# One core: windowed attention and a gated feed-forward layer, its hand-written order of steps replaced by another order of the same steps

## The chip, the cores and the metric

The kernel runs on one core of a Trainium2 chip. The core has a matrix engine (PE, with weight loads listed as PEld), a vector engine (DVE), a scalar engine (ACT), a general engine (POOL) and a queue that requests transfers between device memory and the on-chip memory (SP). Each works through its own instructions in order; they wait for each other by semaphores. The metric is the device time of one execution in microseconds (us), lower is better.

## What is computed

Four batches, 8 heads, 768 positions, 64 values a head. The attention sees the first 4 positions (the sinks) and a window of 128; behind it stands a gated layer of 512 to 1536 to 512.

```python
scores = scale * np.matmul(q, k.transpose(0, 1, 3, 2))
keep = is_sink | in_window
scores = np.where(keep, scores, -1000000000.0)
a = np.exp(scores - max); a = a / (sum + 1e-09)
x = np.matmul(a, v)                                   # 3072 x 512 over all batches
out = (np.maximum(x @ w_gate, 0) * (x @ w_val)) @ w_out
```

## The kernel before

The work is written as small steps, and one text, ORDER, lists all 1039 of them in the order in which they are issued. A step is a name and numbers (`G.0.1.5`); a table, OPS, maps the name to a function. The program issues exactly in this order (`tc.manual_schedule()`), and every engine's queue is what falls to it out of the list. Waits come from data and buffers alone.

Heads go in pairs: pair i (0 to 15) is batch i // 4, heads 2(i % 4) and the next. The steps, with the engine that runs them:

- Requests (SP): `hk.0.h`, `hq.0.h` load half h of keys and queries of pair 0, `kl.i` and `ql.i` those of pair i (384 KB each), `v.w.j` block j of the values of two pairs (w = i // 2; 128 KB, block 6 is 14 rows), `gl.c`, `xl.c`, `ol.c` one of six chunks of w_gate, w_val, w_out (512 KB each). `tk.i`, `tq.i` transpose keys and queries by DMA. `p`, `o` store results. A load into a buffer waits until the buffer's last reader is done: three buffers for keys and for queries, two for values, six of 512 KB for weights and results (`ws`; chunk c of w_gate is in buffer 2c mod 6, of w_val in 2c + 1 mod 6, of w_out in 6 + c mod 6).
- Constants: `sF`, `sE` (memsets on DVE; `sE` clears padding, ones and block 6 of the value buffers), `sI` (identity) and `sM` (bands of the mask) on POOL, `mk.g` and `mb.g` (masks on DVE), `P.n` (n idle matmuls on PE).
- Casts to bf16: `hc`, `kc`, `qc`, `c`, `f`, `gc`, `xc`, `oc` on POOL; with a capital letter (`kC`, `qC`, `cA`, `fA`, `gC`, `xC`, `oC`) and `hE` on ACT; `hD` on DVE. `f` and `fA` copy the sinks' rows.
- Transposes on PE: `HK`, `HQ` (halves of pair 0), `TK.i`, `TQ.i`; their copies out of PSUM `ha`, `hX`, `ka`, `kb`, `qA`, `qB` on ACT and `hx`, `hg`, `kd`, `ke`, `qa`, `qb` on DVE. Pairs 6 and up are transposed by DMA; `od.i` then arranges keys on POOL.
- Scores: `S.i.g` for a third g of the rows (64 rows of PE at a time, two heads beside each other); for pairs 0 to 3 `b.i.g` first adds the mask by a matmul and `B.i.g` the scores. `E.i.g` is the exponential (ACT), `M.i.g` the mask as a product (DVE).
- `Vd.i` sums (PE, 32-column tiles), `t`, `r`, `s`/`sa` (ACT), `R.i` bring the reciprocal of the sums to every row (DVE). `Va.i.part` multiplies by the values (PE, 32-column tiles; part is a column half), `x.i.part` scales into xT (DVE).
- Feed-forward, for batch b, column half g and 128 of the inner width m: `G.b.g.m` and `W.b.g.m` (PE, four matmuls each, line 502) with w_gate and w_val, `u` the relu (ACT, line 509), `h` the product (DVE, line 514). `F.b.t.m0.m1` is the down-projection of 128 rows (PE, line 524), `y` its copy (ACT), `Z.3.5` the last tile in three parts.

PSUM is four pairs of banks; `take` gives a step the pair that has been free longest in the order, so the order sets who waits for whose copy. Four batches follow each other: while PE does the feed-forward of batch b, the attention of batch b + 1 is woven in. PE's matmuls have three forms of tile: 128x128, 64 rows (scores) and 32 columns (`Vd`, `Va`).

In the order before, the first requests are hk.0.0 hk.0.1 hq.0.0 hq.0.1 kl.1 ql.1 v.0.0 v.0.6 kl.2 ql.2, and gl.2 stands ahead of v.1.5 and v.1.4.

Of the kernel before, what the change touches and what calls it, by code (L numbers as in the profile page):

```python
# [55 lines left out]
G.1.1.4 tk.8 y.0.5 x.6.0 G.1.1.5 kl.11 qc.10 u.1.1.5 kc.10 W.1.1.5 v.4.6 W.1.1.4 h.1.1.5 kl.12 tk.10 y.0.4 W.1.1.11
u.1.1.4 G.1.1.3 h.1.1.4 W.1.1.3 u.1.1.11 v.5.1 G.1.0.9 h.1.1.11 kc.11 G.1.0.0 u.1.1.3 G.1.0.7 u.1.0.0 h.1.1.3 G.1.1.0
u.1.1.0 W.1.0.7 W.1.1.0 u.1.0.9 h.1.1.0 u.1.0.7 G.1.1.10 W.1.0.9 h.1.0.9 h.1.0.7 W.1.0.0 W.1.1.10 od.9 v.5.2 u.1.1.10
G.1.1.8 W.1.1.8 h.1.1.10 G.1.0.4 u.1.1.8 W.1.0.4 tq.10 G.1.1.9 h.1.0.0 h.1.1.8 od.8 c.4.2.4 u.1.1.9 u.1.0.4 G.1.0.2
h.1.0.4 G.1.1.7 W.1.1.9 W.1.1.7 u.1.1.7 u.1.0.2 tq.9 h.1.1.9 v.5.5 W.1.0.2 v.4.0 S.8.0 h.1.1.7 h.1.0.2 S.8.2 S.8.1  # L60
G.1.0.10 W.1.0.10 E.8.2 u.1.0.10 h.1.0.10 E.8.1 G.1.0.11 v.4.1 u.1.0.11 W.1.0.11 h.1.0.11 M.8.2 c.5.2.4 G.1.1.2 S.9.2
E.8.0 S.9.0 S.9.1 v.5.0 W.1.1.2 E.9.2 E.9.0 G.1.0.3 E.9.1 W.1.0.3 M.8.0 M.9.2 od.10 ql.11 u.1.0.3 tk.11 v.4.4 G.1.0.1
G.1.1.1 u.1.1.2 M.9.1 h.1.1.2 W.1.0.1 h.1.0.3 u.1.0.1 ql.13 G.1.0.8 G.1.1.6 W.1.1.1 W.1.1.6 h.1.0.1 u.1.1.1 h.1.1.1
kC.12 G.1.0.5 W.1.0.5 qC.11 G.1.0.6 u.1.0.5 c.4.4.7 W.1.0.8 v.5.4 c.5.0.2 u.1.1.6 fA.4.3 M.9.0 M.8.1 u.1.0.8 ql.12
c.4.0.2 h.1.0.5 W.1.0.6 h.1.1.6 tq.11 h.1.0.8 u.1.0.6 h.1.0.6 S.10.0 S.10.1 E.10.0 S.10.2 E.10.1 Vd.8 kl.13 Vd.9
F.1.2.0.8 E.10.2 od.11 F.1.3.0.8 t.4 F.1.3.8.12 S.11.1 kl.14 r.4 S.11.0 S.11.2 s.4 M.10.0 cA.5.4.7 R.9 R.8 F.1.2.8.12
fA.4.5 E.11.1 M.11.1 ql.14 f.4.1 E.11.2 p.0.1 F.1.0.0.8 f.5.3 E.11.0 M.10.1 qC.12 M.10.2 f.5.1 M.11.0 M.11.2 y.1.2
y.1.3 f.5.5 v.6.3 kl.15 F.1.0.8.12 Vd.10 Va.9.0 tk.12 Va.8.0 Va.8.1 x.9.0 Vd.11 Va.9.1 F.1.1.0.8 t.5 F.1.4.0.8 v.6.4
r.5 s.5 qC.13 x.8.0 v.6.2 kc.13 F.1.1.8.12 tq.12 y.1.0 y.1.1 v.6.6 F.1.5.0.8 x.8.1 F.1.5.8.12 Va.11.0 Va.10.0 c.6.2.4
Va.11.1 R.11 x.9.1 Va.10.1 R.10 F.1.4.8.12 v.6.5 x.10.0 x.11.0 x.11.1 G.2.0.7 u.2.0.7 od.12 x.10.1 v.6.1 tk.13 W.2.0.7  # L70
G.2.0.0 G.2.0.3 W.2.0.0 y.1.4 u.2.0.0 h.2.0.0 W.2.0.3 p.0.0 G.2.1.9 c.6.4.7 h.2.0.7 kc.15 u.2.0.3 G.2.0.11 qc.14 y.1.5
sA G.2.1.4 W.2.1.9 u.2.0.11 od.13 v.7.4 u.2.1.4 W.2.0.11 tq.13 h.2.0.11 kC.14 h.2.0.3 u.2.1.9 p.1.0 G.2.1.3 v.7.2
h.2.1.9 W.2.1.4 h.2.1.4 G.2.1.8 G.2.0.4 tk.15 u.2.0.4 u.2.1.3 u.2.1.8 v.7.5 p.1.1 v.6.0 G.2.0.8 tk.14 W.2.1.3 tq.14
h.2.1.3 W.2.1.8 W.2.0.8 u.2.0.8 h.2.0.8 c.6.0.2 W.2.0.4 S.13.2 h.2.1.8 h.2.0.4 S.12.1 E.13.2 G.2.1.2 u.2.1.2 v.7.1
W.2.1.2 h.2.1.2 G.2.1.1 ql.15 E.12.1 S.13.1 S.13.0 W.2.1.1 v.7.6 G.2.0.1 E.13.0 E.13.1 u.2.0.1 G.2.0.9 od.15 W.2.0.1
# [536 lines left out]
```

## Time and profile before

| | |
|---|---|
| median of three runs | 242.9 us (242.54 to 243.76) |
| profiled execution, span | 242.4 us (no other time of its own is listed) |
| busy: PE, PEld, DVE, ACT, POOL | 234.9, 137.1, 133.2, 131.6, 57.9 us |
| DMA | 39.0 MB, mean 161 GB/s |
| granted clock of PE | full in all 40 slices |

The span runs from the first to the last instruction of the one execution that was profiled. Busy times count an engine's instructions; a matmul's end is modelled, so the distance from start to start says more than its length. The page cuts the span in 40 slices of 6.1 us and gives tenths of busy time. The chain is followed back from the last instruction to what released each step. In a timeline row stand start, length, engine, line, operation, output and inputs, count, and in brackets the idle time before it with what ended it. In a window's row stand the window, its length, busy time of PE, PEld, DVE, ACT and POOL with counts, the clock, the DMA engines' share and GB/s.

### The profile page before, as it was taken

The page shows a single profiled execution, that of the slowest core. Times are in us where ns is not written, and L with a number is a line of the kernel's source. Part 1 is how long each engine was busy: PE and PEld are TensorE (multiplying, and loading weights), DVE is VectorE, ACT ScalarE, POOL GpSimd, SP SyncE. Part 2 cuts the span into 40 slices and gives each one's busy share as a digit, 9 for nine tenths or more (in the row PEclk, how much of TensorE's full clock was granted, in tenths as well). Part 3 has the DMA queues.
Part 4 walks back from the last instruction along what each step waited for, and adds up shares of the span by engine and source line. Part 5 has one row for each costly group of instructions (what it writes and reads, how often), then busy time and mean ns, then how long its engine had stood idle before and what let it go on. Part 6 is the DMA issues. An engine that isn't in the chain of part 4 may idle for free.

```text
span 242.4 us, 5536 instructions
## 1 busy us (share of the span) xinstructions
PE 234.9 (97%) x2213; PEld 137.1 (57%) x2213; DVE 133.2 (55%) x268; ACT 131.6 (54%) x254; POOL 57.9 (24%) x106
## 2 busy tenths in 40 slices
PE   7899989999999999999999999999999999999995
...
GB/s 168 329 279 280 346 341 255 314 316 309 182 227 187 167 230 199 191 166 38 224 219 187 206 135 153 23 143 3 0 3 3 29 318 4 0 0 0 3 130 130
DMA packets 88329, 39.00 MB, mean 161 GB/s; under 512 B 73712, under 2 KB 83824, under 8 KB 88304
## 3 DMA queue, kind: packets, MB, share of 16 engines
...
q8 instruction: 17, 0.28, 0.5%
...
## 4 chain that ended last, share of the span: by engine, by line
PE 80%; SPq 7%; DMA 7%; issue 5%; ACT 0%; DVE 0%
PE pp L502 49%; PE pp L524 22%; DMA ws<-in_moe_w_gate_dram 4%; SPq L237 4%; PE pp L404 3%; PE pp L449 3%; DMA vf<-in_v_dram 3%; PE pp L438 2%; SPq L241 2%; SPq L231 1%; SPq L217 1%; PE pp L329 0%; ACT wg L270 0%; DVE ws L549 0%
## 5 line engine op out<-in xcount | busy, mean ns | idle before, releaser
L514 DVE TENSOR_TENSOR hT<-gs,pp 128x378 bf16<-128x378 f32 (+1 forms) x96 | 50.7, 552 | 75.3 <-PE pp L502 52.0
L509 ACT ACTIVATE gs<-pp 128x378 f32<-128x378 f32 (+1 forms) x96 | 44.2, 494 | 53.9 <-PE pp L502 41.5
L502 PE MATMUL pp<-xT,wg 128*128 128x378 bf16 (+1 forms) x384 | 72.4, 326 | 1.0 <-ACT wg L270 1.0
L502 PE MATMUL pp<-xT,wv 128*128 128x378 bf16 (+1 forms) x384 | 71.9, 326 | 0.0
L524 PE MATMUL pp<-wo,hT 128*128 128x512 bf16 x276 | 62.3, 379 | 0.0
L502 PEld LDWEIGHTS <-wg 128*128 128x128 bf16 x384 | 36.9, 98 | 26.7 <-ACT wg L270 1.4
L502 PEld LDWEIGHTS <-wv 128*128 128x128 bf16 x384 | 37.4, 98 | 25.3 <-issue 0.4
L419 ACT ACTIVATE ee<-pp 128x1010 bf16<-128x1010 f32 (+2 forms) x48 | 43.9, 961 | 11.2 <-PE pp L404 10.9
L524 PEld LDWEIGHTS <-hT 128*128 128x128 bf16 x276 | 26.1, 98 | 30.5 <-issue 0.4
L530 ACT COPY ws<-pp 128x512 f32<-128x512 f32 x23 | 13.1, 589 | 26.0 <-PE pp L524 26.0
L425 DVE TENSOR_TENSOR ee<-ee,msk 128x1014 bf16<-128x1014 bf16 (+2 forms) x36 | 25.5, 747 | 1.6 <-ACT ee L419 1.5
L485 DVE STREAM_TRANSPOSE R<-r 128x832 f32<-128x832 f32 x16 | 16.4, 1037 | 5.2 <-ACT r L477 4.7
L262 POOL CAST vn<-vf 128x512 bf16<-128x512 f32 (+1 forms) x18 | 12.6, 715 | 23.7 <-DMA vf<-in_v_dram 23.7
L491 DVE TENSOR_TENSOR xT<-pp,R 128x390 bf16<-128x390 f32 (+1 forms) x32 | 16.1, 546 | 3.8 <-PE pp L449 3.3
L404 PE MATMUL pp<-qT,kE 64*128 64x255 bf16 (+4 forms) x164 | 13.4, 248 | 0.2 <-ACT qT L355 0.2
L449 PE MATMUL pp<-ee,vn 128*32 128x252 bf16 (+6 forms) x512 | 12.6, 241 | 0.1
L254 POOL CAST qn<-qf 128x768 bf16<-128x768 f32 x11 | 9.4, 858 | 13.1 <-DMA qf<-in_q_dram 12.2
L449 PEld LDWEIGHTS <-vn 128*32 128x32 bf16 x512 | 10.9, 96 | 1.9 <-issue 1.1
L290 POOL COPY kO<-kE 128x372 bf16<-128x372 bf16 x10 | 6.0, 596 | 24.5 <-PE pp L404 20.4
L251 POOL CAST kn<-kf 128x768 bf16<-128x768 f32 x11 | 9.1, 824 | 8.1 <-DMA kf<-in_k_dram 7.4
L460 DVE STREAM_TRANSPOSE t<-pp 128x832 f32<-128x832 f32 (+1 forms) x10 | 8.7, 867 | 4.0 <-PE pp L438 3.2
L404 PEld LDWEIGHTS <-kE 64*128 64x128 bf16 x164 | 6.6, 93 | 7.1 <-issue 5.5
...
## 6 DMA issues: line engine op xcount, KB each, us to landing
...
out_dram<-ws SPq DMA_DIRECT2D x10, 512.0 KB, 3.3
ws<-in_moe_w_gate_dram SPq DMA_DIRECT2D x6, 512.0 KB, 7.8
ws<-in_moe_w_val_dram SPq DMA_DIRECT2D x6, 512.0 KB, 7.8
ws<-in_moe_w_out_dram SPq DMA_DIRECT2D x6, 512.0 KB, 5.2
...
```

What stands on the lines that cost most here:

```text
L262: copy(dst[:, j0:j1, :, :].rearrange("p j h d -> p (j h d)"), src[:, j0:j1, :, :].rearrange("p j h d -> p (j h d)"))
L404: mm = lambda h, c0, c1, lhs, rhs, st: on(("S", i, g), "PE", 1 << h, nc.tensor.matmul(out=ps[:, h, c0:c1], lhsT=lhs, rhs=rhs, start=st, st ...
L419: on(("S", i, g), "ACT", 3, nc.scalar.activation(ee[i % NE][:, g, :, 0:n], use(("S", i, g))[:, :, 0:n], Act.Exp, bias=0.0, scale=scale))
L425: nc.vector.tensor_tensor(x, x, msk[:, g, 0:n].unsqueeze(1).to_broadcast([128, 2, n]), op=Alu.mult)
L449: on(("V", i), "PE", 1 << part, nc.tensor.matmul(out=ps[p0:p0 + 32, part, o0:o0 + c1 - c0], lhsT=vn[w % NVN][:, j, h0 + h, d:d + 32], rhs= ...
L485: nc.vector.transpose(out=R[:].rearrange("p s (c e) -> p (s c) e", e=32), in_=r.rearrange("p s c -> p (s c)").unsqueeze(2).to_broadcast([1 ...
L491: on(("V", i), "DVE", 1 << part, nc.vector.tensor_tensor(xT[b % 2][:, p, c0:c1], use(("V", i))[:, part, 0:c1 - c0], held_r[i][:, part, 0:c ...
L502: on(("F", b, g, m), "PE", 1 << which, nc.tensor.matmul(out=ps[:, which, 0:c1 - c0], lhsT=(wg, wv)[which][:, ko, m * 128:(m + 1) * 128], r ...
L509: on(("F", b, g, m), "ACT", 1, nc.scalar.activation(x[:, 0:n], use(("F", b, g, m))[:, 0, 0:n], Act.Relu, bias=0.0, scale=1.0))
L514: on(("F", b, g, m), "DVE", 2, nc.vector.tensor_tensor(hT[:, m, c0:c1], gs[b, g, m][:, 0:c1 - c0], use(("F", b, g, m))[:, 1, 0:c1 - c0], o ...
L524: on(name, "PE", 1 << t % 2, nc.tensor.matmul(out=ps[:, t % 2, :], lhsT=hT[:, m, t * 128:(t + 1) * 128], rhs=wo[:, m, :], start=m == 0, st ...
L530: on(name, "ACT", 1 << t % 2, act_copy(staged(b, t), use(name)[:, t % 2, :]))
```

## The change

ORDER is replaced. No step is added or taken away and no step moves to another engine; every queue gets its steps in another order. The first requests are now hk.0.1 hq.0.1 hk.0.0 hq.0.0 v.0.0 ql.1 v.0.6 kl.1 kl.2 ql.2 kl.3 ql.3, all blocks of the first batch's values stand ahead of gl.2, and steps of the same form stand together on PE in more places. The core of it, as far as the last value block of batch 1:

```diff
@@ -28,69 +28,69 @@
 ZCUT = (0, 256, 384, 512)
 
 ORDER = """
...
-hk.0.0 sF sE P.40 sM hk.0.1 hq.0.0 mk.0 hc.0.0 mk.1 mk.2 hq.0.1 sI mb.1 b.0.1 mb.0 HK.0.0 hE.0.0 HQ.0.0 b.0.0 mb.2 P.3
-hD.0.1 kl.1 ql.1 v.0.0 v.0.6 hc.0.1 HK.0.1 kl.2 ql.2 HQ.0.1 v.0.2 ha.0.0 hx.0.0 hX.0.1 hg.0.1 B.0.0 b.0.2 B.0.1 B.0.2
-E.0.0 kc.1 v.0.1 kl.3 b.1.1 TK.1 ql.3 qc.1 kc.2 qc.2 ke.1 TQ.1 E.0.1 v.0.3 E.0.2 kc.3 b.1.2 qB.1 qA.1 qc.3 v.0.5 Vd.0
-kd.1 t.0.0 B.1.2 B.1.1 v.1.6 TK.2 r.0.0 b.1.0 TQ.2 kl.4 E.1.2 c.0.0.2 B.1.0 ke.2 E.1.1 s.0.0 c.0.2.4 f.0.1 f.0.3 qb.2
-b.2.0 ka.2 qa.2 v.1.1 b.2.2 kc.4 E.1.0 R.0 B.2.2 v.0.4 Vd.1 B.2.0 TK.3 v.1.3 E.2.2 ql.4 c.0.4.7 TQ.3 E.2.0 b.2.1 qA.3
-v.1.0 qB.3 t.0.1 B.2.1 r.0.1 v.1.2 b.3.0 b.3.2 kd.3 f.0.5 s.0.1 ke.3 qc.4 E.2.1 B.3.0 Vd.2 R.1 E.3.0 B.3.2 t.1.2 r.1.2
-c.1.0.2 gl.2 c.1.2.4 Va.0.0 E.3.2 f.1.3 Va.0.1 b.3.1 v.1.5 B.3.1 TK.4 v.1.4 TQ.4 Va.1.0 x.0.1 sa.1.2 gl.1 E.3.1 f.1.1
-x.0.0 c.1.4.7 f.1.5 qA.4 R.2 kb.4 x.1.0 Vd.3 t.1.3 P.2 r.1.3 ka.4 xl.2 xl.1 qB.4 Va.2.0 xl.0 Va.1.1 v.2.1 sa.1.3 x.1.1
-S.4.1 gc.4 S.4.0 gc.5 x.2.0 E.4.0 Va.3.0 gC.2 R.3 x.3.0 Va.2.1 x.2.1 Va.3.1 xc.5 x.3.1 gl.0 S.4.2 G.0.0.4 E.4.2
-G.0.0.2 E.4.1 xc.4 u.0.0.4 G.0.0.5 kl.5 u.0.0.2 u.0.0.5 gl.5 W.0.0.5 G.0.1.5 W.0.0.4 gc.3 M.4.1 gl.4 xC.2 h.0.0.5 xl.5
-W.0.0.2 G.0.1.2 xC.0 gC.0 h.0.0.2 u.0.1.5 h.0.0.4 u.0.1.2 gc.11 W.0.1.2 v.3.1 W.0.1.5 h.0.1.2 xC.1 G.0.1.4 u.0.1.4
-xc.3 v.2.0 gC.10 G.0.1.0 gc.9 G.0.1.3 h.0.1.5 W.0.1.4 u.0.1.0 W.0.1.0 h.0.1.0 u.0.1.3 G.0.0.3 G.0.0.11 xc.10 ql.5
-W.0.0.3 h.0.1.4 kC.5 W.0.1.3 gC.1 TK.5 u.0.0.3 h.0.0.3 xl.4 G.0.0.0 h.0.1.3 kl.7 xl.3 ke.5 W.0.0.0 xC.11 u.0.0.11
-W.0.0.11 qc.5 G.0.1.11 TQ.5 ka.5 h.0.0.11 G.0.1.1 v.2.6 gl.3 qb.5 qa.5 u.0.0.0 gC.8 ol.2 h.0.0.0 W.0.1.11 ql.6 W.0.1.1
-S.5.2 u.0.1.1 u.0.1.11 h.0.1.11 xC.9 S.5.0 h.0.1.1 S.5.1 G.0.1.10 ol.5 E.5.2 M.4.2 G.0.0.8 M.5.2 E.5.0 E.5.1 W.0.1.10
-G.0.0.10 G.0.1.9 W.0.1.9 xC.8 gc.6 u.0.1.10 xC.6 gc.7 u.0.1.9 W.0.0.10 u.0.0.10 h.0.1.9 h.0.1.10 G.0.0.1 kl.6 xc.7
-oc.2 ol.1 h.0.0.10 W.0.0.1 ol.3 G.0.0.9 G.0.1.8 u.0.0.1 h.0.0.1 u.0.0.9 G.0.0.6 qc.6 u.0.0.8 ol.0 W.0.0.9 tq.6 oc.0
-ql.7 W.0.0.8 ol.4 h.0.0.8 kC.6 tk.6 G.0.1.7 h.0.0.9 u.0.0.6 M.5.0 G.0.1.6 W.0.1.6 v.2.4 oC.1 M.5.1 W.0.0.6 W.0.1.8
-u.0.1.6 h.0.0.6 G.0.0.7 h.0.1.6 oC.3 W.0.0.7 u.0.0.7 v.3.5 kc.7 u.0.1.7 M.4.0 cA.2.0.2 W.0.1.7 u.0.1.8 qc.7 oc.5
-h.0.1.7 v.2.2 h.0.0.7 tk.7 Vd.4 Vd.5 v.3.4 od.6 t.2 tq.7 v.2.5 oC.4 v.2.3 od.7 F.0.0.0.8 F.0.1.0.8 S.6.1 h.0.1.8 v.3.0
-E.6.1 S.6.2 S.6.0 r.2 E.6.0 v.3.3 sa.2 F.0.1.8.12 E.6.2 F.0.0.8.12 R.4 F.0.2.0.8 M.6.2 ql.8 c.2.4.7 c.2.2.4 y.0.1
-M.6.0 F.0.2.8.12 y.0.0 v.3.6 M.6.1 y.0.2 fA.2.3 v.3.2 f.2.1 c.3.2.4 S.7.1 E.7.1 S.7.0 kl.9 kl.8 S.7.2 F.0.3.0.8
-F.0.3.8.12 v.4.3 E.7.0 R.5 c.3.0.2 Vd.6 E.7.2 M.7.1 fA.2.5 Va.5.0 cA.3.4.7 Va.4.0 v.4.2 ql.9 y.0.3 M.7.0 fA.3.3 qc.8
-Va.4.1 M.7.2 f.3.1 x.5.0 Vd.7 t.3 f.3.5 x.4.1 F.0.4.0.8 Va.5.1 v.4.5 r.3 v.5.3 Va.7.0 Va.7.1 sa.3 x.5.1 Va.6.0 Va.6.1
-F.0.5.0.8 v.5.6 kc.9 F.0.5.8.12 R.6 x.4.0 R.7 tk.9 kc.8 x.7.0 x.6.1 x.7.1 F.0.4.8.12 qC.9 tq.8 kl.10 ql.10 G.1.1.11
...
+sI hk.0.1 sF sM mk.0 mb.0 hq.0.1 P.40 b.1.0 hk.0.0 hc.0.0 HK.0.0 hq.0.0 hE.0.0 b.0.0 mk.2 mb.2 v.0.0 P.3 hc.0.1 HK.0.1
+ql.1 qc.1 sE hD.0.1 v.0.6 ha.0.0 HQ.0.1 hX.0.1 mk.1 mb.1 HQ.0.0 hx.0.0 kl.1 b.0.2 kl.2 B.0.0 kc.1 hg.0.1 B.0.2 E.0.0
+E.0.2 kc.2 b.0.1 B.0.1 E.0.1 ql.2 b.1.1 qc.2 TK.1 TQ.1 kl.3 kd.1 Vd.0 qA.1 qB.1 ke.1 t.0.0 r.0.0 B.1.0 E.1.0 ql.3 P.2
+kc.3 TK.2 B.1.1 v.0.1 b.2.0 TQ.2 v.0.2 b.1.2 qc.3 B.1.2 ke.2 s.0.0 E.1.1 qb.2 b.2.2 v.0.3 ql.4 c.0.0.2 f.0.1 qa.2
+c.0.2.4 f.0.3 ka.2 B.2.2 B.2.0 R.0 v.1.6 E.1.2 E.2.2 Vd.1 t.0.1 E.2.0 TK.3 r.0.1 kd.3 s.0.1 v.0.4 qc.4 ke.3 TQ.3 qB.3
+b.2.1 B.2.1 v.0.5 b.3.2 qA.3 kl.4 b.3.0 v.1.1 B.3.0 R.1 E.2.1 B.3.2 E.3.0 Vd.2 t.1.2 r.1.2 c.0.4.7 Va.1.0 E.3.2 x.1.0
+Va.0.0 x.0.0 f.0.5 Va.0.1 b.3.1 B.3.1 sa.1.2 E.3.1 x.0.1 kc.4 v.1.0 v.1.2 TK.4 v.1.3 kb.4 ka.4 c.1.0.2 f.1.1 R.2
+c.1.2.4 f.1.3 v.1.5 v.1.4 c.1.4.7 f.1.5 TQ.4 gl.2 qA.4 gc.4 Va.1.1 x.1.1 Vd.3 xl.2 qB.4 t.1.3 r.1.3 Va.2.0 gl.1 x.2.0
+gc.5 Va.2.1 x.2.1 S.4.0 v.3.6 sa.1.3 E.4.0 S.4.2 E.4.2 Va.3.0 Va.3.1 xc.4 R.3 x.3.1 xl.1 S.4.1 x.3.0 M.4.2 G.0.1.5
+G.0.0.4 G.0.0.5 W.0.0.4 u.0.0.4 M.4.0 h.0.0.4 gl.0 xc.5 W.0.1.5 u.0.1.5 h.0.1.5 xl.0 gC.2 gl.5 G.0.1.4 E.4.1 kl.5 xl.5
+W.0.0.5 gc.3 ql.5 v.3.3 xC.2 G.0.1.3 xc.3 u.0.0.5 h.0.0.5 W.0.1.4 G.0.0.2 u.0.1.4 h.0.1.4 gc.11 G.0.1.2 gC.0 u.0.1.2
+v.2.0 W.0.1.2 h.0.1.2 xl.4 W.0.0.2 u.0.0.2 u.0.1.3 W.0.1.3 h.0.1.3 xC.0 G.0.1.0 G.0.0.3 u.0.0.3 W.0.0.3 h.0.0.3
+W.0.1.0 gC.10 G.0.0.0 qc.5 gC.1 h.0.0.2 W.0.0.0 gl.3 xc.10 G.0.0.11 kC.5 u.0.1.0 h.0.1.0 G.0.1.11 TK.5 xC.1 ke.5 xC.11
+W.0.1.11 u.0.1.11 u.0.0.0 xl.3 h.0.0.0 gc.6 u.0.0.11 TQ.5 gl.4 G.0.1.10 qb.5 qa.5 gc.7 h.0.1.11 W.0.0.11 W.0.1.10 ka.5
+S.5.2 xc.7 h.0.0.11 u.0.1.10 h.0.1.10 kl.7 ol.4 ol.5 S.5.0 E.5.2 S.5.1 ql.6 E.5.1 G.0.0.10 G.0.0.1 W.0.0.10 G.0.1.1
+W.0.1.1 xC.6 M.4.1 qc.6 W.0.0.1 M.5.1 u.0.0.1 E.5.0 gc.9 u.0.1.1 h.0.1.1 M.5.2 h.0.0.1 ol.0 v.2.3 gC.8 G.0.1.7 u.0.1.7
+oc.0 W.0.1.7 G.0.0.7 W.0.0.7 u.0.0.7 h.0.0.7 M.5.0 xC.9 G.0.0.6 W.0.0.6 ol.1 u.0.0.6 kl.6 h.0.1.7 xC.8 ol.3 G.0.1.6
+W.0.1.6 ol.2 G.0.1.9 ql.7 u.0.1.6 kc.7 u.0.1.9 h.0.1.6 Vd.4 Vd.5 h.0.0.6 G.0.1.8 u.0.0.10 h.0.0.10 oC.1 G.0.0.9
+W.0.0.9 kC.6 oc.2 tq.6 oC.3 tk.6 t.2 r.2 sa.2 R.5 W.0.1.9 W.0.1.8 v.2.4 G.0.0.8 W.0.0.8 h.0.1.9 u.0.1.8 F.0.0.0.8 oC.4
+tk.7 u.0.0.9 h.0.1.8 u.0.0.8 qc.7 F.0.1.0.8 oc.5 h.0.0.8 od.6 h.0.0.9 F.0.0.8.12 S.6.0 v.3.2 E.6.0 S.6.2 E.6.2 od.7
+S.6.1 F.0.1.8.12 M.6.2 F.0.2.0.8 F.0.2.8.12 v.2.1 cA.2.0.2 E.6.1 y.0.0 y.0.1 v.3.1 tq.7 S.7.0 v.3.0 E.7.0 c.3.0.2
+f.3.1 S.7.1 R.4 S.7.2 E.7.1 M.6.1 v.2.2 F.0.3.0.8 F.0.3.8.12 c.2.2.4 f.2.1 y.0.2 Va.5.0 v.3.4 v.2.6 c.3.2.4 v.2.5
+c.2.4.7 M.6.0 Va.4.0 v.3.5 M.7.1 v.4.1 ql.8 E.7.2 M.7.0 Va.7.0 fA.2.3 fA.2.5 x.5.0 M.7.2 y.0.3 Va.5.1 x.5.1 v.4.2
+cA.3.4.7 fA.3.3 Vd.6 Va.6.0 x.4.0 Va.4.1 x.4.1 Vd.7 t.3 r.3 sa.3 f.3.5 R.6 Va.6.1 x.6.1 Va.7.1 R.7 F.0.4.0.8 F.0.5.0.8
...
 """.split()
```

77 lines of the change are left out of this document (39 added, 38 removed).

## The prediction

> **What bounds the kernel now.** I read the page's shares and slices first, then the chain of waits, then the timelines of the engines over the first 40 us.
>
> ```profile
> span 242.4 us, 5536 instructions
> PE 234.9 (97%) x2213; PEld 137.1 (57%) x2213; DVE 133.2 (55%) x268; ACT 131.6 (54%) x254; POOL 57.9 (24%) x106
> PE   7899989999999999999999999999999999999995
> ```
>
> PE is busy 97%, and full from the seventh slice (36 us) on. Busy alone doesn't prove a limit; the chain does:
>
> ```profile
> 25.23 9.66 DMA ws<-in_moe_w_gate_dram
> 34.91 0.63 ACT wg L270
> 35.59 5.50 PE pp L502 x32
> 182.30 10.47 PE pp L524 x48
> 192.77 29.88 PE pp L502 x184
> ```
>
> From 35.59 us every piece up to the close is PE's. 184 projection matmuls in 29.88 us are 0.1624 us each, 48 of the down-projection in 10.47 are 0.218; the same rates hold throughout, so behind 35.59 there is PE work and changes of tile form, and no stall to remove. All that PE can lose or win otherwise lies before 35.59, where the first batch's attention runs and the weights arrive.
>
> ```profile
> 27.24 2.09 PE L502 MATMUL pp<-xT,wg 128*128 128x378 bf16 x12
> 35.59 1.60 PE L502 MATMUL pp<-xT,wg 128*128 128x390 bf16 x8 [1.03 <-ACT wg L270]
> ```
>
> The up-projection starts at 27.24. By 35.59 it has done 11 groups of four matmuls (G.0.0.4 to G.0.1.4 of the order): 44 x 0.1624 = 7.15 us of work in 8.35. So 1.2 us are lost, all at G.0.1.0, which waits for gl.0, the first 256 columns of w_gate (requested at 25.23, landed 34.89, cast by ACT).
>
> **The change, part by part.** The same 1039 steps stand in another order; I counted and walked them queue by queue.
>
> *Changes of form.* PE alternates 128x128 tiles, 64-row tiles (scores) and 32-column tiles (sums, values). Counted along the order, the changes go from 67 to 58; after the first up-projection group from 38 to 32. The price of one:
>
> ```profile
> 99.66 2.12 PE L502 MATMUL pp<-xT,wv 128*128 128x390 bf16 x12
> 101.72 0.28 PE L404 MATMUL pp<-qT,kE 64*128 64x253 bf16 x2
> L502 PE MATMUL pp<-xT,wv 128*128 128x390 bf16 x192 | 37.6, 328 | 0.0
> ```
>
> The last of the twelve starts at 99.66 + 2.12 - 0.33 = 101.45, its successor in the same form would start 0.165 later, at 101.62; the score starts at 101.72: 0.10 us. Six fewer on the full stretch: -0.6 us. The three fewer ahead of it fall where PE waits anyway: 0.
>
> *The weight wait.* In the new order G.0.1.0 has 14 groups ahead of it, not 11 (+2.0 us of PE work), and gl.0 has 0.65 MB less ahead of it in the request queue (xl.0 and v.2.1 go behind it). It is late no more: -1.2 us. The new v.3.6 ahead of xl.1 on SP waits until POOL has cast batch 0's last values.
>
> ```profile
> 25.07 0.82 POOL L262 CAST vn<-vf 128x768 bf16<-128x768 f32 x1 [1.48 <-DMA vf<-in_v_dram]
> 26.30 1.16 POOL L270 CAST wg<-ws 128x512 bf16<-128x512 f32 x2
> ws<-in_moe_w_gate_dram SPq DMA_DIRECT2D x6, 512.0 KB, 7.8
> ```
>
> That cast and its row of sinks end near 26.3; so xl.1 lands by 26.6 + 7.8 = 34.4, and is wanted eleven groups (7.1 us) after the start at 28.9 (below): 36.0. Covered by 1.6 us less a cast of 0.6.
>
> *The first requests.* This is where the new order pays. SP's new queue is hk.0.1, hq.0.1, hk.0.0, hq.0.0, v.0.0, ql.1, v.0.6, kl.1, kl.2, ql.2, kl.3, ql.3. v.0.6 overwrites rows that sE has cleared on DVE, so it waits for sE. sE ran at once; now it stands behind mk.0, mb.0, mk.2 and mb.2, and mk.0 waits for POOL's bands.
>
> ```profile
> 1.51 0.31 DVE L188 MEMSET kE<- 128x57 uint32 x4
> 1.86 0.55 DVE L191 MEMSET vf<- 128x256 f32 x2
> 3.49 0.16 DVE L198 MEMSET msk<- 4x126 bf16 x1 [0.84 <-POOL msk L179]
> 4.11 0.23 DVE L202 COPY msk<-msk 128x252 bf16<-128x252 bf16 x1
> 4.25 0.31 DVE L204 COPY msk<-msk 128x255 bf16<-128x255 bf16 x1
> 4.98 0.66 DVE L210 TENSOR_SCALAR mb<-msk 128x507 bf16<-128x507 bf16 x3
> 0.81 0.96 SPq L231 DMA_DIRECT2D kf<-in_k_dram  x2
> 2.83 0.47 SPq L217 DMA_DIRECT2D kf<-in_k_dram  x1
> 3.41 0.50 POOL L257 CAST kn<-kf 128x384 bf16<-128x384 f32 x1
> 8.76 0.83 POOL L251 CAST kn<-kf 128x768 bf16<-128x768 f32 x1 [3.83 <-DMA kf<-in_k_dram]
> 10.73 0.51 PE L329 MATMUL pp<-ident,qn 128*128 128x128 bf16 x6 [0.58 <-POOL qn L254]
> ```
>
> From 3.49: mk.0 0.6 (to 4.11), mb.0 and mb.2 a third of 0.66 each, mk.2's copies 0.75 (4.25 to 4.98, with waits 0.9), sE's kE and ones 0.4, the first vf 0.27: v.0.6 can go near 6.1, kl.1 at 6.6 instead of 2.83. Meanwhile the queue holds 1.3 MB. When does kl.1 land? It took 5.9 us (2.83 to 8.76) behind four half loads; the first half load, with nothing ahead, took 2.6 (0.81 to 3.41). A whole load is 0.2 MB more, 0.6 us at the 328 GB/s of 6 to 12 us (below). So 3.2 to 5.9 us, landing between 9.8 and 12.5; I take 4.3, landing at 10.9, nearer the lower end since little is ahead, while kl.2, ql.2 and kl.3 follow at 0.5 us and share the engines. Then the cast 0.83, TK.1 and TQ.1 0.35 each: TQ.1 ends at 12.4, against 11.24 (10.73 + 0.51). Delay 1.2 us. Does it pass on?
>
> ```profile
> 6.00:12.00 6.00, 4.90 (x66) 2.80 (x65) 2.87 (x9) 4.61 (x11) 2.04 (x3) 1.00 1.11 328
> 12.00:18.00 6.00, 5.64 (x78) 3.08 (x76) 5.59 (x17) 5.53 (x10) 3.90 (x6) 1.00 1.05 281
> 18.00:24.00 6.00, 5.85 (x119) 3.40 (x120) 5.64 (x14) 5.74 (x15) 5.43 (x11) 1.00 0.98 276
> 25.85 1.05 DVE L485 STREAM_TRANSPOSE R<-r 128x832 f32<-128x832 f32 x1
> 27.00 1.49 DVE L491 TENSOR_TENSOR xT<-pp,R 128x378 bf16<-128x378 f32 x3
> ```
>
> It does. From 12 us DVE (third column) and ACT (fourth) are busy over 92%, in nearly the old order: what starts late ends late. In addition x.2.1 now stands ahead of R.3 on DVE, and the first group is of the second column half, which needs x.3.1 behind R.3: 0.5 us (27.00's three take 1.49). Start of the up-projection: 27.24 + 1.2 + 0.5 = 28.9: +1.7 us. gl.2, whose casts took 26.30 to 27.46, has the last two values ahead of it and the later start; 1.4 us are covered. sI ahead of the bands fits POOL's idle 0.8 us; b.1.0 0.5 us sooner, hk.0.1 ahead of hk.0.0 and B.0.0 0.8 us later sit before ACT's wait for TQ.1: 0.
>
> The Trainium skill, "DMA: Bandwidth & Descriptors", section "Anatomy of one DMA", puts a load at about 2.0 us plus its bytes at 436 GB/s (fitted on another path): an estimated 2.9 us for kl.1, landing at 9.5, where it would delay nothing, and a sum of -0.3 where mine is +0.9. No load in these rows is that quick; by it the faster rival below would be near.
>
> *w_out.* ol.3 takes the staging buffer that xC.8 empties, xC.8 stands behind u.0.0.6 on ACT, and ol.2, ql.7 and both transposes stand behind ol.3 on SP. So ol.3 and ol.2 are requested only when PE has done G.0.0.6: 37 groups x 0.65 + 1.6 for transposes and scores after the start = 54.6, plus relu 0.5 and cast 0.6: 55.7 and 56.2.
>
> ```profile
> ws<-in_moe_w_out_dram SPq DMA_DIRECT2D x6, 512.0 KB, 5.2
> 57.97 1.46 POOL L274 CAST wo<-ws 128x1024 bf16<-128x1024 f32 x1 [6.02 <-DMA ws<-in_moe_w_out_dram]
> ```
>
> Landing 5.2 later and 1.46 of cast: 62.9. F.0.0 starts at 28.9 + 48 x 0.65 + 2.6 (transposes, scores, sums, changes) = 62.7 and uses that chunk four matmuls (0.9) later: covered by 0.7. With the gate weights' 7.8 us it would be late by 1.9. I take 0.3. tk.6 behind them lands in time for S.6.0 by under 1 us: 0.
>
> *Dense blocks.* Fewer changes mean that values and sums of four pairs stand in one block, with no down-projection between to cover DVE.
>
> ```profile
> 72.00:84.00 12.00, 11.98 (x200) 6.90 (x198) 11.30 (x17) 6.71 (x14) 5.03 (x7) 1.00 1.10 177
> L419 ACT ACTIVATE ee<-pp 128x1010 bf16<-128x1010 f32 (+2 forms) x48 | 43.9, 961 | 11.2 <-PE pp L404 10.9
> L425 DVE TENSOR_TENSOR ee<-ee,msk 128x1014 bf16<-128x1014 bf16 (+2 forms) x36 | 25.5, 747 | 1.6 <-ACT ee L419 1.5
> L485 DVE STREAM_TRANSPOSE R<-r 128x832 f32<-128x832 f32 x16 | 16.4, 1037 | 5.2 <-ACT r L477 4.7
> L491 DVE TENSOR_TENSOR xT<-pp,R 128x390 bf16<-128x390 f32 (+1 forms) x32 | 16.1, 546 | 3.8 <-PE pp L449 3.3
> 78.19 1.75 PE pp L449 x75
> ```
>
> Batch 1, from the end of S.7.0 to the next up-projection: PE has 0.5 of scores, 36 down-projections x 0.218 = 7.8, 128 value matmuls at 1.75/75 = 3.0, two sums 0.8, changes 0.3: 12.4 us. The other chain is two exponentials 1.9, three masks 2.2, six x's 3.3, t and r 1.5, ACT's copies of r 0.9, two R 2.1: 11.9, and some 0.5 of hand-overs. They are level, and DVE was busy 11.3 of 12 there already: the cover is gone, and what comes late shows in full. Three such blocks, 0 to 0.5 each: I take 0.5 in all. Everything else that moves (stores, casts, later loads) lies beside full PE: 0. The close is the same.
>
> **Sum.** -0.6 - 1.2 + 1.7 + 0.3 + 0.5 = +0.7; with 0.2 for weights that may now gate the start, +0.9. The span is 242.4, 0.5 under the median of 242.9; against the median 243.8.
>
> **Rivals.** *Late refill (slower).* kl.1 lands at 12.5, as slowly as before. Start +3.3, w_out +0.8, blocks +0.6: -1.8 + 4.7 = +2.9, 245.8. For it: the row 8.76; against: little is ahead. It decides from a landing after 11.3. *Quick refill (faster).* kl.1 lands at 9.8, start +0.6, no later stalls: -1.8 + 0.6 = -1.2, 241.7. For it: the first half load's 2.6 us; against: three followers sharing. *Blocks stall (slower).* DVE, not PE, ends each of three blocks, 1 us each: +2.6, 245.5; for it DVE's 11.3 of 12.
>
> **How the numbers follow.** Forecast 0.45 (243.8, own range 242.6 to 244.8), late refill 0.28, quick refill 0.19, blocks 0.08. Range 241.9 to 246.2. About 0.5% (1.2 us) can be told from no change: below 241.7, above 244.1. Faster: 0.13 of the quick case. Same: 0.30 of the forecast, 0.06 of the quick case, 0.05 of the others. Slower: the rest, 0.46.
>
> **What will show it.** The second k load's request on SP after 6 us and the first whole-k cast near 10.9; the first up-projection near 28.9 instead of 27.24; no wait for wg behind it; under 0.5 us of PE idle at F.0.0 and at the ends of the value blocks. I am wrong if the start stays below 28, or if PE idles over 1 us anywhere after 36.

## The result, and the profile after

The new order is slower: median 245.72 us (244.87 to 246.89, six runs) against 242.72 (242.29 to 243.76, six runs), a ratio of 1.0114 with the interval 1.0082 to 1.0146. The profiled execution of after has a span of 244.0 and a time of 245.72 of its own, a typical one (six spans from 243.1 to 245.2, median 243.95); in every kernel of this study the time lies 1.7 to 1.9 us above the span.

The kernel before doesn't take the same time twice: over the study its executions had spans of 240.3 to 244.0, and its profiled execution of 242.4 was a long one; one execution of 245.7, at a granted clock of 0.993, is left out as disturbed. The median of before also shifts with the round in which it is measured (242.7, 243.0, 243.0 and, in the last round, 243.95), so a kernel's ratio is taken to before in its own round.

The page of after, and PE's busy tenths in the 40 slices:

```profile
span 244.0 us, 5518 instructions
PE 234.8 (96%) x2202; PEld 138.4 (57%) x2213; DVE 132.7 (54%) x268; ACT 131.9 (54%) x254; POOL 57.6 (24%) x106
PE   7789899999998999999999999999999999999995
```

PE has the same work (eleven of its records are missing, so x2202). But its row has an 8 in the middle where before has nines only, and the chain of waits (start, length, what) no longer runs through PE alone from 36 us on:

```profile
28.48 0.57 DVE xT L491
...
29.10 12.76 PE pp L502 x78
41.86 0.51 ACT wv L270
42.39 5.13 DMA ws<-in_moe_w_val_dram
...
47.58 0.63 POOL wv L270
...
48.55 6.63 DMA qf<-in_q_dram
...
55.30 0.83 POOL qn L254
56.13 0.57 POOL wg L270
...
57.14 6.68 DMA qf<-in_q_dram
...
75.02 1.87 DVE ee L425
...
76.93 0.81 PE pp L449 x32
...
85.25 20.88 PE pp L502 x128
...
238.52 2.67 PE pp L547 x36
```

Between 42 and 77 us it goes through weight and query loads, POOL and a mask product on DVE. From 85.25 on it is PE's again. PE's busy time in the two windows that hold this, and the rows of its timeline:

```profile
48.00:60.00 12.00, 11.53 (x98) 6.84 (x97) 6.27 (x11) 7.92 (x15) 3.34 (x5) 1.00 1.10 318
72.00:84.00 12.00, 10.97 (x202) 6.61 (x200) 9.42 (x14) 6.41 (x14) 5.88 (x9) 1.00 1.15 212
```

```profile
11.35 0.51 PE L329 MATMUL pp<-ident,kn 128*128 128x128 bf16 x6 [1.04 <-ACT ee L419]
11.69 0.50 PE L329 MATMUL pp<-ident,qn 128*128 128x128 bf16 x6
...
28.39 2.31 PE L502 MATMUL pp<-xT,wg 128*128 128x390 bf16 x12 [0.32 <-ACT ee L419]
...
55.45 0.82 PE L502 MATMUL pp<-xT,wv 128*128 128x390 bf16 x4
56.75 0.83 PE L502 MATMUL pp<-xT,wg 128*128 128x390 bf16 x4 [0.47 <-POOL wg L270]
...
75.38 0.73 PE L449 MATMUL pp<-ee,vn 128*32 128x253 bf16 x24
76.93 0.81 PE L449 MATMUL pp<-ee,vn 128*32 128x253 bf16 x32 [0.82 <-DVE ee L425]
```

The brackets count from a modelled end; from start to start more is lost. Four matmuls of 0.165 from 55.45 end at 56.11, the next group (G.0.1.9) starts at 56.75: 0.64 us. 24 value matmuls at 1.75 / 75 us from 75.38 end at 75.94, the next (Va.7.0) starts at 76.93: 1.0 us.

So, against the profiled execution of before (+1.6 of span): the up-projection starts 1.15 later (28.39, was 27.24), the weight wait of 1.2 is gone, G.0.1.9 costs 0.6 and Va.7.0 1.0; six changes of form fewer are worth 0.5 (at the price measured below). That is +1.05. The rest, some 0.5, are small waits of 0.1 to 0.2 each, the largest at 28.7 (the first group for x.3.0), 64.6 and 72.6.

SP shows where the query loads of the chain became late:

```profile
5.64 0.39 SPq L237 DMA_DIRECT2D vf<-in_v_dram  x1
6.07 0.89 SPq L217 DMA_DIRECT2D kf<-in_k_dram  x2
...
34.82 1.38 SPq L241 DMA_DIRECT2D ws<-in_moe_w_val_dram  x1
40.76 0.37 SPq L241 DMA_DIRECT2D ws<-in_moe_w_gate_dram  x1
...
48.55 0.46 SPq L220 DMA_DIRECT2D qf<-in_q_dram  x1
```

From 36.2 to 40.8 it stands still: gl.3 waits for its buffer, which the ACT cast gC.1 empties at 40.7. Everything behind gl.3 waits with it. It isn't gC.1 that moved: 19 groups of the up-projection stand ahead of it in both orders, and in before it ended at 39.9. What moved is the queue. In before gl.3 stood behind xl.4, kl.7, xl.3 and v.2.6, and ql.6 two places further on was requested at 44.72. Now gl.3 stands directly behind xl.4. Five requests come between it and ql.6 (xl.3, gl.4, kl.7, ol.4, ol.5), and xl.3 waits for xC.1, which has 22 groups ahead of it instead of 10. So ql.6 goes out at 48.55.

### The profile page after: what moved, and what is told of

Its sections match the earlier page's. It is cut to its first block, busy times and chain, and to the rows that moved or that the text cites. A ratio compares the mean times of both kernels' runs of the same rounds, so it can differ in the third digit from the quotient of the medians.

```text
span 244.0 us, 5518 instructions
## 1 busy us (share of the span) xinstructions
PE 234.8 (96%) x2202; PEld 138.4 (57%) x2213; DVE 132.7 (54%) x268; ACT 131.9 (54%) x254; POOL 57.6 (24%) x106
## 4 chain that ended last, share of the span: by engine, by line
PE 74%; DMA 10%; ACT 5%; DVE 5%; issue 2%; POOL 2%; SPq 1%; DVEq 0%; POOLq 0%; ACTq 0%
PE pp L502 44%; PE pp L524 20%; DMA qf<-in_q_dram 5%; ACT ee L419 3%; PE pp L449 3%; PE pp L404 3%; DMA ws<-in_moe_w_val_dram 2%; PE pp L438 2%; DMA kf<-in_k_dram 1%; DMA vf<-in_v_dram 1%; PE pp L547 1%; DVE t L460 1%; DVE ee L425 1%; DVE R L485 1%; POOL qn L254 1%
## 5 line engine op out<-in xcount | busy, mean ns | idle before, releaser
L509 ACT ACTIVATE gs<-pp 128x378 f32<-128x378 f32 (+1 forms) x96 | 45.1, 493 | 56.9 <-PE pp L502 50.6
L502 PE MATMUL pp<-xT,wg 128*128 128x378 bf16 (+1 forms) x384 | 73.6, 326 | 0.8 <-POOL wg L270 0.5
L502 PE MATMUL pp<-xT,wv 128*128 128x378 bf16 (+1 forms) x384 | 73.3, 325 | 0.0
L524 PE MATMUL pp<-wo,hT 128*128 128x512 bf16 x265 | 60.6, 379 | 0.7 <-issue 0.2
L419 ACT ACTIVATE ee<-pp 128x1010 bf16<-128x1010 f32 (+2 forms) x48 | 44.4, 966 | 10.9 <-PE pp L404 7.4
L425 DVE TENSOR_TENSOR ee<-ee,msk 128x814 bf16<-128x814 bf16 (+2 forms) x36 | 25.4, 726 | 12.4 <-ACT ee L419 12.2
L491 DVE TENSOR_TENSOR xT<-pp,R 128x378 bf16<-128x378 f32 (+1 forms) x32 | 16.1, 545 | 0.6
L262 POOL CAST vn<-vf 128x512 bf16<-128x512 f32 (+1 forms) x18 | 13.5, 757 | 5.4 <-DMA vf<-in_v_dram 5.4
L404 PE MATMUL pp<-qT,kE 64*128 64x255 bf16 (+4 forms) x164 | 14.2, 248 | 0.5 <-issue 0.2
L449 PEld LDWEIGHTS <-vn 128*32 128x32 bf16 x512 | 11.6, 96 | 1.8 <-DVE ee L425 1.0
```

The lines of the kernel that those rows point to most:

```text
L262: copy(dst[:, j0:j1, :, :].rearrange("p j h d -> p (j h d)"), src[:, j0:j1, :, :].rearrange("p j h d -> p (j h d)"))
L404: mm = lambda h, c0, c1, lhs, rhs, st: on(("S", i, g), "PE", 1 << h, nc.tensor.matmul(out=ps[:, h, c0:c1], lhsT=lhs, rhs=rhs, start=st, st ...
L419: on(("S", i, g), "ACT", 3, nc.scalar.activation(ee[i % NE][:, g, :, 0:n], use(("S", i, g))[:, :, 0:n], Act.Exp, bias=0.0, scale=scale))
L425: nc.vector.tensor_tensor(x, x, msk[:, g, 0:n].unsqueeze(1).to_broadcast([128, 2, n]), op=Alu.mult)
L449: on(("V", i), "PE", 1 << part, nc.tensor.matmul(out=ps[p0:p0 + 32, part, o0:o0 + c1 - c0], lhsT=vn[w % NVN][:, j, h0 + h, d:d + 32], rhs= ...
L491: on(("V", i), "DVE", 1 << part, nc.vector.tensor_tensor(xT[b % 2][:, p, c0:c1], use(("V", i))[:, part, 0:c1 - c0], held_r[i][:, part, 0:c ...
```

## The experiments

Twelve kernels, each an edit of ORDER. Their medians are compared with those of before and after; for the shares of a microsecond the spans and the traces are used.

**Before, once more.** No edit.

> The kernel before, unchanged, to learn whether its profiled execution was a typical one. After lasts 1.7 us longer than its span (245.72 against 244.0); if that holds before too, its median of 242.72 belongs to a span of 241.0, not 242.4. Theory A: the wait of 1.2 us at G.0.1.0 is in every execution; it shows again at 1.0 to 1.3 us and the span is 242.4 within 0.3. Rival B: the profiled execution was a long one; the span is near 241.0, the wait at G.0.1.0 is under 0.4 us, and the change had nothing to win there.

Median 244.11 (12 runs), ratio to before 1.0038 (1.0006 to 1.0070): the kernel against itself shows what 0.4% is worth here. Spans from 241.2 to 244.0, the profiled one 243.0. Its PE timeline:

```profile
34.12 2.25 PE L502 MATMUL pp<-xT,wg 128*128 128x390 bf16 x12
...
65.61 0.28 PE L404 MATMUL pp<-qT,kE 64*128 64x255 bf16 x2 [0.59 <-DMA kE<-kn]
66.30 0.28 PE L404 MATMUL pp<-qT,kO 64*128 64x252 bf16 x2 [0.41 <-POOL kO L291]
```

G.0.1.0 doesn't wait at all (twelve matmuls in one row, where before had eight behind a wait of 1.03); instead pair 6's transposed keys are late for S.6. So rival B in its main point: the wait that the change was to remove is in one of the two traces of before. The median that the change is measured against, 242.72, is a span of 241.0, 1.4 under the profiled 242.4, so most of those executions can hardly have had a wait of this size; no trace shows them.

**The cast of ql.6 later.**

```diff
-xC.6 M.4.1 qc.6 W.0.0.1 M.5.1 u.0.0.1 E.5.0 gc.9
+xC.6 M.4.1 W.0.0.1 M.5.1 u.0.0.1 E.5.0 gc.9 qc.6
```

> After, with the cast of the seventh query load (qc.6) moved on POOL from ahead of the w_gate cast gc.9 to behind it. In after PE waits 0.6 us at G.0.1.9, which uses gc.9. Theory A: gc.9 only stood behind qc.6, whose load was late; then gc.9 runs near 50 us instead of 56, PE waits under 0.1 us there, and the span falls by 0.6 to 243.4 (ratio to after 0.9975). Rival B: the chunk of w_gate itself (gl.4) is late; then the wait stays at 0.4 us or more. Rival C: the wait goes, but a later one takes its place (transposed keys of pair 6 for S.6.0, near 66 us), and the span stays within 0.2 of 244.0.

The wait at G.0.1.9 is gone (its group starts at 55.95, 0.66 behind the last), and the span is 244.1, the median 245.85: nothing won. PE now waits 0.7 at S.7.0 for a PSUM pair that an exponential frees; that exponential stands on ACT behind a value cast, which begins only at 70.0, when its load has landed. Rival C. A late queue shows at the next place.

**Va.7.0 later.**

```diff
-E.7.2 M.7.0 Va.7.0 fA.2.3 ... Vd.6 Va.6.0 x.4.0
+E.7.2 M.7.0 fA.2.3 ... Vd.6 Va.6.0 Va.7.0 x.4.0
```

> After, with the value step Va.7.0 moved on PE behind Va.6.0, 64 matmuls later in the same block of 32-column tiles, so that no change of form is added. In after PE waits 0.84 us at Va.7.0 for a mask product on DVE. Theory A (order): only Va.7.0 was placed too early; the wait falls under 0.2 us and the span to 243.2. Rival B (the blocks rival of the prediction): DVE ends the block, whatever PE does first; then PE waits 0.6 to 0.9 us at a later value step or at the first up-projection of batch 1, and the span stays within 0.3 of 244.0.

Median 246.08, profiled span 243.4, but the median of its spans is 244.35. The wait is split, 0.36 and 0.40 at 75.7 and 76.1. Rival B: a place in the order doesn't remove it.

**sE early.**

```diff
-sI hk.0.1 sF sM mk.0 mb.0 ... ql.1 qc.1 sE hD.0.1 v.0.6
+sI hk.0.1 sF sE sM mk.0 mb.0 ... ql.1 qc.1 hD.0.1 v.0.6
```

> After, with sE (memsets on DVE) back at its old place, ahead of the masks. Theory A (the first-requests step of the prediction): v.0.6 no longer waits behind the masks, kl.1 is requested near 3.3 instead of 6.1 and cast near 9, the first up-projection starts near 27.3 instead of 28.4, nothing behind it waits more than before, and the span falls by 1.1 to 242.9. Rival B: the weights gate the start by then; the up-projection starts earlier but waits in its first 12 us for casts of w_gate or w_val as much as it started earlier, and the span stays within 0.3 of 244.0. Rival C: kl.1 lands when it did, since more loads share the engines from the start; the start stays above 28.

Median 245.75. kl.1 is requested at 4.43 instead of 6.07, its cast begins at 9.99 instead of 10.46, pair 1's first transpose starts at 10.96 and the up-projection at 28.00. The kernel with the later cast of ql.6, which has after's beginning, had 10.82 and 27.87: no gain. In six kernels of this study with after's first requests unchanged the cast began at 9.67 to 10.16, so the earlier request brought no earlier landing: rival C.

**kl.1 first.** With sE early, as in the kernel above, and kl.1, ql.1 ahead of v.0.0; kc.1 ahead of qc.1.

```diff
-v.0.0 P.3 hc.0.1 HK.0.1 ql.1 qc.1 hD.0.1 v.0.6 ... kl.1 b.0.2 kl.2 B.0.0 kc.1
+kl.1 ql.1 v.0.0 P.3 hc.0.1 HK.0.1 kc.1 qc.1 hD.0.1 v.0.6 ... b.0.2 kl.2 B.0.0
```

> After, with the first requests in the old order behind the halves: kl.1 and ql.1 ahead of v.0.0 and v.0.6 (sE early too, and kc.1 ahead of qc.1 on POOL). With sE early alone kl.1 was requested at 4.4 instead of 6.1, but pair 1's first transpose started at 10.96, against 11.35 in after and 10.82 in a second kernel with after's beginning: the request time did not set it. Theory A: what is ahead of kl.1 in the queue sets it; with kl.1 fifth, as before, pair 1's first transpose starts near 9.7, its first exponential near 12.4 and the up-projection at 27.4 (after and its variants so far: 27.9 to 28.5). Rival B: the masks, which now stand later on DVE, set the pace; the first exponential of pair 1 stays above 12.9 and the up-projection above 28.

Median 245.50. POOL's timeline, here and in after, and PE's here:

```profile
7.50 0.83 POOL L251 CAST kn<-kf 128x768 bf16<-128x768 f32 x1 [1.01 <-DMA kf<-in_k_dram]
```

```profile
10.46 0.83 POOL L251 CAST kn<-kf 128x768 bf16<-128x768 f32 x1 [2.01 <-DMA kf<-in_k_dram]
```

```profile
10.89 0.49 PE L329 MATMUL pp<-ident,kn 128*128 128x128 bf16 x6 [0.15 <-ACT ee L419]
11.22 0.50 PE L329 MATMUL pp<-ident,qn 128*128 128x128 bf16 x6
...
27.93 2.31 PE L502 MATMUL pp<-xT,wg 128*128 128x390 bf16 x12 [0.66 <-ACT ee L419]
```

The cast is 3 us earlier than in after, and the transposes move by 0.5 only. The order gives TK.1 the PSUM pair that pair 0's second exponential (E.0.2) frees; in the order before it was the first one's (E.0.0). Here that second exponential ends at 10.84 and TK.1 starts at 10.89. In after it ended at 10.41, the cast of kl.1 at 11.29, and TK.1 started at 11.35: there the cast was the limit, though the bracket names an exponential; the last one (E.0.1, to 11.32) isn't needed by TK.1, which here started long before that one ended (11.75). So neither theory in full: kl.1 was the limit in after, and with kl.1 early the first pair is, half a microsecond sooner. Of the ten traces with the new first pair, TK.1 starts 0.05 or 0.06 behind that cast in four (after among them) and as closely behind that exponential in six. From TQ.1 (11.22) to the up-projection (27.93) it is 16.7 us, as in after (11.69 to 28.39); it is 16.7 or 16.8 in nine of the fourteen traces and 16.5 to 17.7 in the others.

**Early casts.**

```diff
-gC.0 u.0.1.2 ... xC.0 G.0.1.0 ... qc.5 gC.1 h.0.0.2 ... TK.5 xC.1 ke.5
+gC.0 gC.1 u.0.1.2 ... xC.0 xC.1 G.0.1.0 ... qc.5 h.0.0.2 ... TK.5 ke.5
```

> After, with the ACT casts gC.1 and xC.1 (second halves of the first chunks of w_gate and w_val) moved directly behind gC.0 and xC.0, so that their buffers come free earlier; nothing else. In after SP stands still from 36.2 to 40.8, waiting for gC.1 before it can request gl.3, and everything behind on SP is late with it. Theory A: this is the source of the waits between 55 and 77 us (G.0.1.9, S.6, S.7, and the value casts on POOL that slow the masks ahead of Va.7.0): gl.3 goes out by 37.5, ql.6 by 46, each of these waits falls under 0.3 us, and the span falls by 1.5 or more, to 242.5. Rival B: the waits at G.0.1.9 and the scores go, but the wait of 1.0 at Va.7.0 stays above 0.7, as it belongs to the dense block: span 243.2.

The one clear gain: median 244.47, ratio to before 1.0066 (1.0050 to 1.0082), 1.25 us under after (1.03 under the kernel before this one, which ran in the same round), and the twelve spans (242.4 to 243.1) all lie at or under the shortest of after. Its SP and PE timelines:

```profile
35.20 1.31 SPq L241 DMA_DIRECT2D ws<-in_moe_w_gate_dram  x1
...
44.65 0.46 SPq L220 DMA_DIRECT2D qf<-in_q_dram  x1
```

```profile
55.57 0.82 PE L502 MATMUL pp<-xT,wg 128*128 128x390 bf16 x4
...
75.40 0.81 PE L449 MATMUL pp<-ee,vn 128*32 128x253 bf16 x32 [0.83 <-DVE ee L425]
```

gl.3 goes out at 35.2 (was 40.8), ql.6 at 44.7 (48.6), and between the first group and 75 us PE waits no more. The wait at Va.7.0 stays as it was. Rival B in the waits; the median span, 242.7, is nearer to what theory A said. In this kernel gC.1 stands behind 11 groups, earlier than in either order, so this is more than taking a move back.

**The down-projection back in the block.** F.0.4.0.8 in Va.7.0's place, Va.7.0 behind x.4.1.

```diff
-M.7.0 Va.7.0 fA.2.3 ... x.4.1 Vd.7 ... Va.7.1 R.7 F.0.4.0.8 F.0.5.0.8
+M.7.0 F.0.4.0.8 fA.2.3 ... x.4.1 Va.7.0 Vd.7 ... Va.7.1 R.7 F.0.5.0.8
```

> After, with the down-projection F.0.4.0.8 (8 matmuls, 1.73 us) put back inside the value block of batch 1, where Va.7.0 stood, and Va.7.0 three steps later: two changes of form more. Theory A (dense blocks): the cover is back, the wait of 0.8 to 1.0 us at Va.7.0 falls under 0.2 us, and the span falls by 0.8 less 0.2 for the two changes, to 243.4. Rival B: DVE ends the block in any order; with Va.7.0 later in the same block and no cover PE still waited 0.76 in two pieces, and here 0.5 or more appears behind the block, at the first up-projection of batch 1.

Median 247.90, worse. Its PE timeline:

```profile
85.45 0.33 PE L502 MATMUL pp<-xT,wg 128*128 128x390 bf16 x1 [1.23 <-DVE xT L491]
...
239.06 2.81 PE L547 MATMUL pp<-wo,hT 128*128 128x256 bf16 x36 [0.67 <-ACT ws L530]
```

No wait inside the block, but 1.2 us behind it for the last x: DVE ends this stage whatever stands first on PE. The moved step also takes another PSUM pair, which shifts the pairs of all steps behind it; the wait before the last tile probably comes from that. So this run speaks for rival B, with a second effect mixed in. The profiled execution, 244.7, is one of the two shortest of six (median 246.2); what the others lose besides isn't shown.

**All three together.** The edits of the last three kernels.

> After with the three edits together: first requests as before, the two casts early, the down-projection in the block. If the three terms add, it has no wait over 0.3 us on PE and its start is that of before, so its span is that of before without waits (240.8 in before's quickest executions) less the fewer changes of form, 0.4 to 0.5 us: 240.4, median 242.1. If the terms are one cause, it equals the variant with early casts alone within 0.3 us.

Median 246.25. PE waits 1.2 at the up-projection of batch 1 and again before the last tile, as in the run above. The terms don't add: the third is a loss, and the first won nothing.

**The old first pair.** Early casts, and the first 53 steps of the order before. In this kernel and in the one with both edits below, the two idle matmuls of P.2 write over 128 columns of PSUM pair 3 while it holds a mask block of pair 1, so a part of that mask is lost and pair 1's output is partly wrong; all steps are there.

> The variant with early casts (gC.1, xC.1; median span of its executions 242.7), and in addition the first 53 steps of the order before, up to TQ.1; then the rest as in after. With kl.1 and its cast early alone, pair 1's transposes did not move (10.89 against 10.8 to 11.35): they stand on PE behind all three scores of pair 0 and wait for its exponentials, and pair 0's first score starts at 8.2 in after, 7.2 before. Theory A: this first pair is what delays the start, not the second k load; with the old first steps the first score starts at 7.2 to 7.5, TK.1 at 9.7, the up-projection at 27.2 (27.9 without), span 242.0. Rival B: DVE and ACT, busy over 90% from 12 us on, set the start whatever stands ahead; the up-projection stays at 27.8 or above and the span at 242.7.

Median 244.28, spans from 241.2 to 244.1 (median 242.5; 242.7 without, in another round). Against before in its own round the ratio is 1.0024 (0.9996 to 1.0052), so it can't be told from before; early casts alone had 1.0066. Its shortest is 1.2 under the shortest of early casts alone; in the profiled one, the longest, PE waits for the casts of the first loads:

```profile
10.19 0.51 PE L329 MATMUL pp<-ident,kn 128*128 128x128 bf16 x6 [0.54 <-POOL kn L251]
11.36 0.51 PE L329 MATMUL pp<-ident,qn 128*128 128x128 bf16 x6 [0.66 <-POOL qn L254]
...
28.10 2.10 PE L502 MATMUL pp<-xT,wg 128*128 128x390 bf16 x10
```

Again 16.7 us from TQ.1 to the start. With the same beginning, the kernel with both edits has TQ.1 at 9.96 and starts at 26.75, the two traces of before 27.24 and 27.63. So with the old first pair the loads set TQ.1 (9.96 to 11.36): the first exponential, whose PSUM pair TK.1 takes there, ends at 8.7 to 9.4. With the new one TQ.1 starts at 11.14 or later, as the second exponential ends at 10.2 to 11.0. On average the four traces with the old first pair start at 27.4, the ten with the new one at 28.2. That is theory A in the mean; by this trace alone (28.10, over the 27.8 of rival B) it would be B.

**Values early.** Early casts, and v.2.1, v.2.2, v.2.4 to v.2.6, v.3.0 to v.3.2, v.3.4 and v.3.5 ahead of ol.3.

> The variant with early casts, and in addition ten loads of batch 1's values (w = 2 and 3) moved on SP ahead of ol.3, where SP stood waiting from 49.6 to 54.9. Every mask product that took over 0.70 us in the three traces compared (before twice, after) had a POOL cast beside it; the 63 without one took at most 0.692. Theory A (the casts slow the masks): the values are cast by 72 us, the masks of pair 7 take 0.7 us each instead of 0.9 and 1.9, the wait of 1.0 us at Va.7.0 falls under 0.3, span 241.8. Rival B (exponentials): ACT gives pair 7's last exponential late, and the wait stays at 0.6 or more. Rival C: the loads displace the ones of w_out or the transposes of pair 6, and PE waits at F.0.0 or at S.6.0 instead.

Median 251.84: rival C in the time, theory A in the block. PE's timeline and windows, then DVE's and POOL's timelines:

```profile
68.04 5.30 PE L524 MATMUL pp<-wo,hT 128*128 128x512 bf16 x16 [4.91 <-POOL wo L274]
...
80.98 1.36 PE L449 MATMUL pp<-ee,vn 128*32 128x253 bf16 x56
```

```profile
70.00:72.00 2.00, 2.00 (x7) 0.74 (x6) 0.21 (x1) 0.00 (x0) 1.62 (x8) 0.57 0.81 156
72.00:74.00 2.00, 2.00 (x21) 0.88 (x18) 0.00 (x0) 0.29 (x1) 1.35 (x3) 1.00 0.00 0
```

```profile
79.96 1.29 DVE L425 TENSOR_TENSOR ee<-ee,msk 128x1014 bf16<-128x1014 bf16 x2 [1.07 <-ACT ee L419]
```

```profile
76.37 1.37 POOL L262 CAST vn<-vf 128x512 bf16<-128x512 f32 x2
82.98 0.39 POOL L266 CAST vn<-vf 4x256 bf16<-4x256 f32 x1 [5.24 <-ACT vn L262]
```

ol.3 and ol.2 are now requested at 60.0, and the down-projection waits 4.9 us for w_out. But POOL has no cast between 77.7 and 83.0, the two masks of pair 7 at 79.96 take 1.29 together, and Va.7.0 doesn't wait (56 value matmuls in one row). Its block lies 3.4 us behind S.7.0 (77.57), as in early casts alone (70.42 to 73.84), so the wait at w_out gave the masks no more time. In early casts alone the same two, beside POOL's casts, take:

```profile
72.81 2.54 DVE L425 TENSOR_TENSOR ee<-ee,msk 128x1014 bf16<-128x1014 bf16 x2 [1.75 <-ACT ee L419]
```

1.25 us more, and PE waited 1.0. This is the cause of the wait at Va.7.0.

**Both edits.** The old first pair and the values early.

> Both edits of the two kernels above on the variant with early casts. If their terms add (0.7 for the start, 1.0 for the value block), no wait over 0.3 us is left on PE, the span is 241.0 and the median 242.7, with executions as close together as those of early casts alone (0.7 us). That would equal before's median and leave out its slow executions (up to 243.9 of span).

Median 250.89. The start is the earliest of all (26.75), so w_out is missed by more (6.2 us).

**Sixteen changes of form more.** Early casts, and eight steps one place into the next block: W.1.1.8, W.1.1.2, W.1.0.8, F.1.1.8.12, W.2.1.1, W.2.1.5, W.2.1.10, W.2.1.0; h steps behind their W.

```diff
-W.1.1.8 ... S.8.0 S.9.1
+S.8.0 W.1.1.8 ... S.9.1
```

> The variant with early casts, and in addition eight matmul groups (seven W and one F of batches 1 and 2) moved one place into the block of scores or sums behind them: 16 changes of tile form more, 48 instead of 32 behind the first up-projection group, the same matmuls. At 0.10 us for a change, as the prediction had it, the span grows by 1.6 to 244.3; at 0.05 us by 0.8 to 243.5. Rival: changes cost nothing where PE's queue is full, span 242.7.

Median 246.60. Its profiled execution lost time ahead of batch 1, where nothing is changed, so the price is read from the start of batch 1 on, where all sixteen lie. (Its span is 247.6; the other five have 243.9 to 245.5.) The chain of early casts, then that of this kernel, each with the first projections of batch 1 and the last tile:

```profile
83.61 20.88 PE pp L502 x128
...
236.88 2.67 PE pp L547 x36
```

```profile
87.43 20.22 PE pp L502 x124
...
242.16 2.66 PE pp L547 x36
```

153.27 and 154.73 us between them: 1.46 for sixteen, 0.09 us a change. In after it is 153.27 as well (85.25 to 238.52). By the medians, each against before in its own round (1.0103 and 1.0066), it is 0.9 us, 0.06 a change. One caution: in both traces of before this stretch takes 153.41, only 0.14 more than in after, though it has four changes more (26 and 22); inside its blocks of scores and sums the new order loses most of that again.

## Why the prediction was right and wrong

Slower was the likeliest sign, and 245.72 lies in the range; the forecast of 243.8 and its own range to 244.8 missed. The range reached that far because of rivals whose mechanisms did not come, so that it held is in part luck. Of the signs, the request, the cast, the start and F.0.0 came nearly as put; "no wait for wg behind it" and "under 0.5 us" at the ends of the value blocks did not (0.6 and 1.0, which also just reaches "PE idles over 1 us anywhere after 36"). By its steps:

- **Changes of form, -0.6.** The price was right: 0.09 us a change measured, 0.5 for six. The gain was not had in full: 0.14 for four from batch 1 on.
- **The weight wait, -1.2.** Right for the profiled execution, and wrong as a term against the median: the second trace of before has no such wait. "The span is 242.4, 0.5 under the median" was the mis-sized step: a time lies 1.7 above its span, so the median of 242.72 is a span of 241.0, too short to have the wait in it as a rule. The predicted span, 242.4 + 0.9 = 243.3, is 0.7 under the measured 244.0; the other 1.2 us of the error is this.
- **The first requests, +1.7.** v.0.6 went at 5.64 (said 6.1), kl.1 at 6.07 (6.6), its cast began at 10.46 (10.9), TQ.1 ended 0.95 later than before (1.2), the start came at 28.39 (28.9). That a late TQ.1 passes on in full is confirmed by the constant 16.7 us. The 0.5 for x.3.1 behind R.3 doesn't show: from TQ.1 to the start it took 16.5 and 16.9 in the two traces of before. In after's own trace the cause was the one put, kl.1's late cast. What the step left out is the second limit behind it: "hk.0.1 ahead of hk.0.0 and B.0.0 0.8 us later sit before ACT's wait for TQ.1: 0". TK.1 now needs the second exponential of pair 0, and that alone holds it at 10.8 to 11.1 in six of ten traces. With kl.1 cast 3 us earlier the start came 0.5 earlier, not 1.15.
- **w_out, +0.3.** Not needed: PE doesn't wait at F.0.0. That its cover is thin is shown by the values-early run, where requests 5 us later cost 4.9.
- **"Everything else that moves (stores, casts, later loads) lies beside full PE: 0".** This failed. gl.3 moved up on SP to where its buffer wasn't yet empty, xC.1 went back on ACT, five requests came between gl.3 and ql.6; SP stood for 4.6 us, and ql.6 was late; its cast held gc.9 on POOL. Casting gC.1 and xC.1 earlier won 1.25 us of the median, the largest gain found.
- **Dense blocks, +0.5.** Right in kind, larger in one place: 1.0 in batch 1's block, none in the other two in after's trace. DVE does end the block, as the sum of 11.9 against 12.4 had it, but the masks were counted at 0.74 us each and one took 1.9.
- **The rivals.** The time came out at late refill's 245.8 for other reasons: kl.1 landed at 10.4, not 12.5. Blocks stall happened once instead of three times. The page of the Trainium skill, "DMA: Bandwidth & Descriptors", section "Anatomy of one DMA", gave an estimated 2.9 us for kl.1; from request to cast it took 4.4 (6.07 to 10.46), and 3.6 to 4.1 in six other traces with the same first requests, so here the measurement decides against it, as the prediction had taken it.

Open: how much of the 1.15 us at the start belongs to the first pair and how much to kl.1 can't be split from these runs, since the old beginning varies by 1.4 us from one execution to the next. No version that beats before was found.
